# A third width for the first layer of an expert's unit: 128 columns when the unit holds one slot

## The chip, the cores and the metric

The kernel runs on one core of a Trainium2 chip. The metric is device time in microseconds (us), the median of a few executions. A core has TensorE (PE; its weight loads are listed apart as PEld), VectorE (DVE), ScalarE (ACT), GpSimd (POOL), a queue engine (SP), and 16 DMA engines. Each engine runs its own instruction stream in order, branches included; semaphores order the engines among each other.

## The reference

Three steps: a gated recurrence over time, a dense layer that takes the maximum of three products, and a layer that sends each of the 3072 tokens to one of eight experts.

```python
for t in range(S):                                   # recurrence, per batch and head
    state = alpha[:, :, t, :, None] * state + np.einsum('bhd,bhe->bhde', k[:, :, t], v[:, :, t])
    y[:, :, t] = np.einsum('bhd,bhde->bhe', q[:, :, t], state)

h = np.maximum(np.maximum(x @ w1, x @ w2), x @ w3)   # dense layer, 384 -> 768 -> 384
x = h @ w_out

e_idx = np.argmax(x @ w_gate, axis=1)                # experts, 384 -> 1024 -> 384
for e in range(E):
    mask = e_idx == e
    h = np.maximum(x[mask] @ w1[e], 0.0)
    out[mask] = gate_w[mask, None] * eom[mask, e, None] * (h @ w2[e])
```

The change touches the first product of the experts alone, `x[mask] @ w1[e]`.

## The kernel before

The first 446 us compute the recurrence and the dense layer; the change leaves them as they are. After them stands the expert layer. The tokens of an expert are cut into units of 256 tokens, held in slots of 128. The program is written for 20 units (`NU`), of which units 0 and 1 stand outside any branch, units 2 to 9 always run (`NV` is 10), and units 10 to 19 run only if the input has that many; `turn(u)` (L1447) calls the next turn inside a branch on the number of units (L1485), so that a run with fewer units jumps from the last one to the end of the program.

What an expert's last unit holds is its *kind*, worked out at run time (`units_e`, L876) and loaded into a register of each engine by `load_meta` (L925). Kind 0 is two slots (256 columns). Kind 2 is two slots and a rest of up to 64 tokens (256 + 64 = 320 columns). Kind 3 is a unit with at most 128 tokens: one slot. A rest that has no full unit before it is done elsewhere (`own`, L1095).

A turn of unit `u` does, in the order of each engine's program: the first layer `up(u)` (L1036); the split of the expert's second weights into a high and a low part, if the expert is new (`split2`, L676: ACT writes `w2H`, DVE subtracts and writes `w2L`); the gathers, transposes and first-weight splits for the next unit (skipped if there is none, L1465); the second layer of slot 0, `down_tile(u, 0)` (L1069); a tiny expert (`own`) in the turns of units 2 to 9; then the second layer of slot 1 and of the rest, `down_rest` (L1090), which for kind 3 is replaced by a one-column filler matmul into `psN` (`nothing`, L997). GpSimd then sends the finished rows to the output with an indirect DMA (`send`, L1039; `put`, L1043).

The first layer makes the 1024 hidden values in eight blocks `f` of 128. For each block, `up_one` (L1014) runs nine matmuls into one bank of PSUM: three slices of the 384 inputs, times the products high*high, high*low and low*high of weights and tokens, all in the single-pass type fp32r.

```python
        for k in range(3):
            for m, (w, x) in enumerate(((w1H, hi), (w1H, lo), (w1L, hi))):
                mm(ps, w[:, k, f * 128:(f + 1) * 128], x[:, k, :n], start=(k + m == 0), stop=(k + m == 4))
```

The weights stand still in the array (128 x 128, loaded anew for each matmul) and `n` columns of tokens stream past. `cut` (L1023) then applies the ReLU on ACT (L1024) and takes the low part on DVE (L1027). PSUM banks for these blocks come from a pool of three (`psM`). After block 2 stands the first piece of the split of the second weights, in a branch of its own (L1034, L1440).

Before the change a unit's first layer has two arms, chosen by `by_kind` (L1001): kind 2 takes 320 columns, every other kind takes 256. In the program the arm with 320 stands first, so units of kind 0 and 3 jump over it. A branch is an instruction of every engine that loaded the register: PE, ACT, DVE and POOL.

Of the kernel before, what the change touches and what calls it, by code (L numbers as in the profile page):

```python
# [24 lines left out]
DM, FF1, NE, FF2 = 384, 768, 8, 1024  # L25
# [14 lines left out]
LAST = 64  # L40
# [48 lines left out]
def layers(tc, pool, wk, K, general, *args):  # L89
    with ExitStack() as ctx:  # L90
        _layers(ctx, tc, pool, wk, K, general, *args)


def _layers(ctx, tc, pool_, wk, K, general, qk, al, a0, v, vT, w123, wout, gates, ew1, ew2, out):
# [547 lines left out]
    xg, cx, gate, chg, fetched, eos, kind = ({} for _ in range(7))  # L642
# [358 lines left out]
    def by_kind(u, arms, rest):  # L1001
        if not arms or u not in kind:
            return rest()
        (n, f), *more = arms.items()
        with tc.If(kind[u] == n) as c:  # L1005
            f()
        with c.Else():
            by_kind(u, dict(more), rest)
# [5 lines left out]
    def up_one(u, n, f):  # L1014
        hi, lo = cx[u % 2]
        w1H, w1L = C["w1"]
        ps = bank(psM, "M", "psM1")[:, :n]
# [3 lines that stand above are left out]
        return ps  # L1021

    def cut(ps, n, f):  # L1023
        nc.scalar.activation(chid(0, f, slice(0, n)), ps, AF.Relu)  # L1024
        for a, b, to in ((0, min(n, 256), 384), (256, n, 320)):
            if a < b:
                nc.vector.scalar_tensor_tensor(C["h"][f // 4][:, f % 4, to:to + b - a], ps[:, a:b], 0.0,  # L1027
                                               chid(0, f, slice(a, b)).bitcast(F32), op0=ALU.max, op1=ALU.subtract)

    def up_some(u, n, fs, split=False):  # L1030
        for f in fs:
            cut(up_one(u, n, f), n, f)
            if split and f == 2:
                fresh(u, split2, range(2))  # L1034

    def up(u):  # L1036
        by_kind(u, {2: lambda: up_some(u, 256 + LAST, range(NE), True)}, lambda: up_some(u, 256, range(NE), True))

    def send(y, p, c):  # L1039
        nc.gpsimd.indirect_dma_start(out=out[:, :], out_offset=bass.IndirectOffsetOnAxis(ap=sidx[:p, c:c + 1], axis=0),  # L1040
# [128 lines left out]
    if not general:  # L1169
# [90 lines left out]
        for i in range(3, NBLK):  # L1260
            order = batches if i > 3 else [(c, b) for b in (1, 0) for c in range(CPB)]
            n = len(order)
            d = (starts[i + 1] - starts[i]) / n
# [175 lines left out]
    def fresh(u, split, *a):  # L1439
        with tc.If(chg[u] == 1):  # L1440
            split(u, *a)
# [5 lines left out]
    def turn(u):  # L1447
# [4 lines left out]
        if u + 2 < NU:  # L1452
            load_expert(u + 2)
        up(u)
        fresh(u, split2, range(2, NE))
        if u == NF:
# [87 lines left out]
```

## Time and profile before

| | |
|---|---|
| median of 3 runs | 717.69 us (716.19 to 717.78) |
| the profiled execution's own time | 715.22 us |
| its span, first to last instruction | 713.5 us |
| PE, PEld busy | 692.7 us (97%), 655.0 us (92%) |
| DVE, ACT, POOL busy | 392.7 us, 288.7 us, 122.7 us |
| last unit's first layer on PE | 687.55 to 695.72 us |
| last unit's second layer on PE | 695.86 to 700.50 us |
| start of the last send on POOL | 704.77 us |

The page counts PE busy while any of its pipelined matmuls is under way, so the spacing of starts says more than the busy share: 72 matmuls of 256 columns, each 0.28 us long by itself, start within 8.17 us. A weight load is 0.19 us long, and loads overlap matmuls and each other. Rows that end in "xN" merge N instructions; the time beside them is from the first start to the last end.

### The profile page before, as it was taken

The numbers are of one execution on the slowest core, as the hardware profiler recorded it, in microseconds if no ns is written. First come the engines' busy times: TensorE is split into PE (matmuls) and PEld (weight loads), VectorE is DVE, ScalarE is ACT, GpSimd is POOL, SyncE is SP. The second block draws the span as 40 slices with busy tenths as digits, with TensorE's granted clock in tenths as the row PEclk, the third lists the DMA queues.
The fourth block names the chain that finished last, engine by engine and source line by source line (L and its number), as shares of the span: only waits on it lengthen the run. The fifth ranks groups of instructions, "written<-read, shape, count | busy, mean of one in ns | idle before, by whom it ended". The sixth has DMA issues, their size and how long they took to land. (4 is left out here: it accounts for less than half of the span.)

```text
span 713.5 us, 13995 instructions
## 1 busy us (share of the span) xinstructions
PE 692.7 (97%) x5097; PEld 655.0 (92%) x5097; DVE 392.7 (55%) x897; ACT 288.7 (40%) x755; POOL 122.7 (17%) x136
## 2 busy tenths in 40 slices
PE   8999999999999999999999999999999999999992
PEld 8888999999999999999999999999878899999992
DVE  7868887476955736826324365872215264225461
ACT  4345442555733533524323214333325364234451
POOL 1000000001111110111111114052132243332320
PEclk9999999999999999999999999999999999999997
DMA  9905310561510510500000015026566342135330
GB/s 248 380 24 182 107 60 1 147 192 46 152 43 13 138 42 21 131 34 9 13 23 10 22 30 226 23 69 233 196 223 228 121 137 61 58 97 178 128 131 21
DMA packets 23019, 74.88 MB, mean 105 GB/s; under 512 B 7915, under 2 KB 12085, under 8 KB 19841
## 3 DMA queue, kind: packets, MB, share of 16 engines
q1 hardware_dynamic: 17376, 60.95, 26.2%
q0 software_dynamic: 4384, 11.72, 5.2%
q8 instruction: 55, 0.90, 0.5%
q10 hardware_dynamic: 1152, 0.89, 0.5%
q14 instruction: 52, 0.42, 0.2%
HBM read 100.67 MB, written 9.94 MB: 155 GB/s over the span
## 5 line engine op out<-in xcount | busy, mean ns | idle before, releaser
L1020 PE MATMUL psM<-cx,w1H 128*128 128x256 f32 (+1 forms) x576 | 110.1, 290 | 0.0
L489 POOL TENSOR_TENSOR hL<-hm,hH 128x384 fp32r<-128x384 f32 x36 | 38.6, 1072 | 387.6 <-ACT hH L484 387.5
L463 PE MATMUL hps<-xH,wH 128*128 128x384 f32 x432 | 103.7, 347 | 0.4 <-ACT hm L467 0.2
L463 PE MATMUL hps<-xH,wL 128*128 128x384 f32 x432 | 98.5, 335 | 1.6 <-DVE wL L432 1.6
L1077 PE MATMUL psP<-w2H,ch 128*128 128x384 f32 x368 | 99.0, 340 | 0.2 <-issue 0.2
L463 PE MATMUL hps<-xL,wH 128*128 128x384 f32 x432 | 98.5, 335 | 0.0
L1020 PEld LDWEIGHTS psM<-cx,w1H 128*128 128x128 f32 x576 | 91.1, 188 | 0.2
L1027 DVE SCALAR_TENSOR_TENSOR ch<-psM,ch 128x256 fp32r<-128x256 f32 (+1 forms) x128 | 44.6, 371 | 82.5 <-ACT ch L1024 71.8
L1020 PE MATMUL psM<-cx,w1L 128*128 128x256 f32 (+1 forms) x288 | 83.3, 289 | 0.0
L463 PEld LDWEIGHTS hps<-xH,wH 128*128 128x128 f32 x432 | 74.1, 188 | 5.6 <-ACT hm L467 1.2
L463 PEld LDWEIGHTS hps<-xH,wL 128*128 128x128 f32 x432 | 76.9, 188 | 2.3 <-DVE wL L432 2.3
L463 PEld LDWEIGHTS hps<-xL,wH 128*128 128x128 f32 x432 | 77.2, 188 | 0.3 <-DVE xL L375 0.3
L1077 PEld LDWEIGHTS psP<-w2H,ch 128*128 128x128 f32 x368 | 66.8, 188 | 2.8 <-issue 2.1
L503 PE MATMUL ops<-wo,hH 128*128 128x400 f32 x258 | 68.2, 345 | 0.0
L470 DVE TENSOR_TENSOR hm<-hm,hps 128x384 f32<-128x384 f32 x48 | 26.4, 550 | 69.0 <-PE hps L463 55.4
L1024 ACT ACTIVATE ch<-psM 128x256 fp32r<-128x256 f32 (+1 forms) x96 | 38.3, 401 | 62.9 <-PE psM L1020 57.1
L1077 PE MATMUL psP<-w2L,ch 128*128 128x384 f32 x184 | 61.7, 335 | 0.1
L484 ACT CAST hH<-hm 128x384 fp32r<-128x384 f32 x43 | 22.0, 512 | 87.9 <-DVE hm L473 84.1
L1020 PEld LDWEIGHTS psM<-cx,w1L 128*128 128x128 f32 x288 | 54.5, 189 | 0.0
L1040 POOL DMA_INDIRECT out<-yo,sidx x27 | 29.5, 1092 | 113.5 <-ACT yo L1088 24.5
L503 PEld LDWEIGHTS ops<-wo,hH 128*128 128x128 f32 x258 | 47.2, 188 | 0.4
L503 PE MATMUL ops<-wo,hL 128*128 128x400 f32 x129 | 44.4, 344 | 0.0
(263 smaller groups left out, 1108.6 us busy)
## 6 DMA issues: line engine op xcount, KB each, us to landing
s1a<-in_ew SPq DMA_DIRECT2D x12, 1536.0 KB
s2a<-in_ew SPq DMA_DIRECT2D x12, 1536.0 KB
s1b<-in_ew SPq DMA_DIRECT2D x8, 1536.0 KB
s2b<-in_ew SPq DMA_DIRECT2D x8, 1536.0 KB
ws<-in_w SPq DMA_DIRECT2D x6, 1152.0 KB
at<-in_al SPq DMA_DIRECT2D x16, 336.9 KB
vt<-in_v SPq DMA_DIRECT2D x8, 576.0 KB
x2d<-xs SPq DMA_DIRECT2D x24, 192.0 KB
```

The costliest lines, as they stand in the source:

```text
L463: mm(ps, slab(a, f)[:, w, k], b[i][:, k], start=(n == 0), stop=(n == 8))
L470: nc.vector.tensor_max(m, m, ps)
L484: nc.scalar.copy(hH[i, f], m)
L489: (nc.gpsimd if not general and i > 1 else nc.vector).tensor_sub(hL[i, f], hps["m"], hH[i, f].bitcast(F32))
L503: mm(ps[:, :DM + NG], a[i, f][:, ts_], wo[f // 3][:, b, f % 3], start=(f + n == 0), stop=(f + n == 7))
L1020: mm(ps, w[:, k, f * 128:(f + 1) * 128], x[:, k, :n], start=(k + m == 0), stop=(k + m == 4))
L1024: nc.scalar.activation(chid(0, f, slice(0, n)), ps, AF.Relu)
L1027: nc.vector.scalar_tensor_tensor(C["h"][f // 4][:, f % 4, to:to + b - a], ps[:, a:b], 0.0, chid(0, f, slice(a, b)).bitcast(F32), op0=ALU.m ...
L1040: nc.gpsimd.indirect_dma_start(out=out[:, :], out_offset=bass.IndirectOffsetOnAxis(ap=sidx[:p, c:c + 1], axis=0), in_=y[:p], in_offset=Non ...
L1077: mm(ps[:, :DM], chid(x, f, slice(128 * t, 128 * t + 128)), w[:, f], start=(f + n == 0), stop=(f == NE - 1 and n == 2))
```

## The change

`up` no longer uses `by_kind`. It has three arms, written out as two nested branches: kind below 2 takes 256 columns and stands in front; in the other branch kind 2 takes 320 columns, and what is left, kind 3, takes 128.

```diff
     def up(u):
-        by_kind(u, {2: lambda: up_some(u, 256 + LAST, range(NE), True)}, lambda: up_some(u, 256, range(NE), True))
+        if u not in kind:
+            return up_some(u, 256, range(NE), True)
+        with tc.If(kind[u] < 2) as c:
+            up_some(u, 256, range(NE), True)
+        with c.Else():
+            with tc.If(kind[u] == 2) as d:
+                up_some(u, 256 + LAST, range(NE), True)
+            with d.Else():
+                up_some(u, 128, range(NE), True)
```

A matmul of the new arm has the same weights and the same number per block; it streams `x[:, k, :128]` in place of `x[:, k, :256]`, and `cut` handles 128 columns on ACT and DVE. The second layer of kind 3 reads slot 0 alone, in both versions. Lines from 1043 on stand nine lower in the changed file.

On ACT, in the turn of unit 11, where the arm with 320 columns ends; the names are PSUM banks of the first layer (`psM`), the hidden values (`ch`), and the staged and the split second weights (`s2a`, `w2H`). Before:

```order
L1024 ACTIVATE ch<-psM_9711 128x320
L1005 UNCONDITIONAL_BRANCH
L1024 ACTIVATE ch<-psM_9724 128x256
L1024 ACTIVATE ch<-psM_9736 128x256
L1024 ACTIVATE ch<-psM_9748 128x256
L1440 COMPARE_AND_BRANCH
L669 CAST w2H<-s2a 128x384 x2
```

and with the change:

```order
L1024 ACTIVATE ch<-psM_10731 128x320
L1043 UNCONDITIONAL_BRANCH
L1024 ACTIVATE ch<-psM_10744 128x128
L1024 ACTIVATE ch<-psM_10756 128x128
L1024 ACTIVATE ch<-psM_10768 128x128
L1449 COMPARE_AND_BRANCH
L669 CAST w2H<-s2a 128x384 x2
```

Behind the arm with 320 columns there now stands an arm with 128 in place of the one with 256; the split after block 2 keeps its place in it.

On PE, the same turn, the seam behind the first arm (`w1H`, `w1L` are the high and low first weights, `cx` the transposed tokens). Before:

```order
L1020 MATMUL psM_9711<-cx,w1H 128x320 x2
L1020 MATMUL psM_9711<-cx,w1L 128x320
L1005 UNCONDITIONAL_BRANCH
L1020 MATMUL psM_9724<-cx,w1H 128x256 x2
L1020 MATMUL psM_9724<-cx,w1L 128x256
```

and with the change:

```order
L1020 MATMUL psM_10622<-cx,w1H 128x256 x2
L1020 MATMUL psM_10622<-cx,w1L 128x256
L1040 UNCONDITIONAL_BRANCH
L1043 COMPARE_AND_BRANCH
L1020 MATMUL psM_10635<-cx,w1H 128x320 x2
L1020 MATMUL psM_10635<-cx,w1L 128x320
```

The arm with 256 now comes first, a second comparison stands behind it, and the unconditional branch at its end leads past two arms, where the branch at the end of the first arm led past one.

## Rows read from the trace of the kernel before

**Rows 1.** The page: busy time, share of the span, instructions of each engine.

```profile
PE 692.7 (97%) x5097; PEld 655.0 (92%) x5097; DVE 392.7 (55%) x897; ACT 288.7 (40%) x755; POOL 122.7 (17%) x136
```

**Rows 2.** PE, groups by form: line, operation, shapes, count, busy us, mean ns.

```profile
L1077 PE MATMUL psP<-w2H,ch 128*128 128x384 f32 x368 | 99.0, 340 | 0.2 <-issue 0.2
L1020 PE MATMUL psM<-cx,w1H 128*128 128x256 f32 x384 | 67.8, 280 | 0.0
L1077 PE MATMUL psP<-w2L,ch 128*128 128x384 f32 x184 | 61.7, 335 | 0.1
L1020 PE MATMUL psM<-cx,w1H 128*128 128x320 f32 x192 | 42.3, 308 | 0.0
```

**Rows 3.** Timeline of PE, the last unit: start us, us, instruction.

```profile
687.55 0.39 PE L1020 MATMUL psM<-cx,w1H 128*128 128x256 f32 x2
...
695.72 0.28 PE L999 MATMUL psN<-ident 128*128 128x1 f32 x2
695.86 0.42 PE L1077 MATMUL psP<-w2H,ch 128*128 128x384 f32 x1
...
697.40 0.44 PE L1077 MATMUL psP<-w2L,ch 128*128 128x384 f32 x1
```

**Rows 4.** Timeline of ACT and DVE, the last unit.

```profile
695.97 0.38 ACT L1024 ACTIVATE ch<-psM 128x256 fp32r<-128x256 f32 x1 [0.65 <-PE psM L1020]
696.25 2.57 ACT L669 CAST w2H<-s2a 128x384 fp32r<-128x384 f32 x6
700.75 0.58 ACT L1088 ACTIVATE yo<-psP,gate 128x384 f32<-128x384 f32 x1 [1.93 <-PE psP L1077]
689.85 0.82 DVE L1027 SCALAR_TENSOR_TENSOR ch<-psM,ch 128x256 fp32r<-128x256 f32 x2 [0.29 <-issue]
696.38 0.42 DVE L1027 SCALAR_TENSOR_TENSOR ch<-psM,ch 128x256 fp32r<-128x256 f32 x1 [0.61 <-ACT ch L1024]
696.78 2.90 DVE L670 TENSOR_TENSOR w2L<-s2a,w2H 128x384 fp32r<-128x384 f32 x6
```

**Rows 5.** Waits from 695 to 713 us: who waited for whom, us, times, longest.

```profile
POOL out L1040 <- ACTq L1485: 10.6, 1, 10.6
```

**Rows 6.** Timeline of PEld: weight loads of 128 columns beside few streaming columns.

```profile
99.87 0.74 PEld L448 LDWEIGHTS gps<-gt,wT 128*128 128x128 f32 x6 [0.40 <-ACT wT L440]
695.60 0.31 PEld L999 LDWEIGHTS psN<-ident 128*128 128x128 f32 x2
```

**Rows 7.** PE and PEld, groups by form: what bounds the new matmul.

```profile
L448 PE MATMUL gps<-gt,wT 128*128 128x16 f32 x36 | 4.6, 255 | 0.4 <-ACT wT L440 0.3
L1012 PE MATMUL psM<-s1b,xF 128*64 128x256 f32 x72 | 8.4, 383 | 0.0
L1083 PEld LDWEIGHTS psP<-w2L,ch 128*64 128x64 f32 x32 | 4.3, 134 | 0.0
L448 PEld LDWEIGHTS gps<-gt,wT 128*128 128x128 f32 x36 | 4.6, 191 | 1.0 <-ACT wT L440 1.0
```

**Rows 8.** ACT and DVE, groups by form: the cuts of the first layer.

```profile
L1024 ACT ACTIVATE ch<-psM 128x320 fp32r<-128x320 f32 x32 | 14.0, 438 | 24.9 <-PE psM L1020 23.9 <-ACT ch L1024 0.9
L1024 ACT ACTIVATE ch<-psM 128x256 fp32r<-128x256 f32 x64 | 24.3, 383 | 38.0 <-PE psM L1020 33.2 <-PE psT L981 2.2 <-ACT ch L1024 2.0
L1027 DVE SCALAR_TENSOR_TENSOR ch<-psM,ch 128x256 fp32r<-128x256 f32 x96 | 40.4, 423 | 82.5 <-ACT ch L1024 71.8 <-ACTq L1440 6.2 <-issue 3.0
L1027 DVE SCALAR_TENSOR_TENSOR ch<-psM,ch 128x64 fp32r<-128x64 f32 x32 | 6.8, 214 | 0.0
```

**Rows 9.** Branches of L1005 (684.8 to 687 us; all) and L1485: ns min/median/max, starts.

```profile
L1005 PEldq COMPARE_BRANCH  x1: 332/332/332, 685.3 to 685.3; - x1
L1005 PEldq COMPARE_BRANCH  x35: 66/207/431, 479.8 to 700.3; - x35
L1485 PEldq COMPARE_BRANCH  x4: 76/128/3489, 661.8 to 704.3; - x4
```

**Rows 10.** The page: a queue of instruction fetches, packets, MB, share of 16 engines.

```profile
q8 instruction: 55, 0.90, 0.5%
```

## Prediction

> **What bounds the kernel now.** I read the page first: TensorE is busy for 97% of the span and no other engine for more than 55% [rows 1]. So a change counts where it alters when TensorE finishes. Then the groups by form, to see how often the new arm will be taken. The 256-column rows of the high weights number 384, the 320-column rows 192 [rows 2]; a first layer has 48 of them (8 blocks, 3 slices, two products), so 8 units took 256 columns and 4 took 320. The second layer of slots 0 and 1 shows 368 + 184 = 552 matmuls [rows 2]; a slot takes 24, so 23 slots ran where 12 units have 24. Exactly one unit did one slot, and only that one enters the new arm.
>
> Which one, the timeline of the end tells [rows 3]: the last first layer is 256 columns wide, 687.55 to 695.72 us, and is followed by one slot of second layer and no other. The unit with one slot is the last of the program, so what its first layer gains or loses stands near the end, with no later unit to hide it.
>
> Then I followed that end through ACT and DVE [rows 4]. The last cut on ACT starts at 695.97; the six casts of the second weights follow it from 696.25, the six subtractions on DVE from 696.78 to 699.68. TensorE begins the second layer at 695.86, and has to take up again at 697.40 when the first of these subtractions has ended. ACT scales the result at 700.75. The last send goes at 704.77, and the waits put it down to ACT's branch at L1485 [rows 5], the jump over the unused turns. So the path is: last first layer on PE, cut and casts on ACT, subtractions on DVE, second layer on PE, scaling, far jump, send. It moves as a whole with the end of the last first layer.
>
> **The change part by part.** *The 72 matmuls of the last unit.* They start over 695.72 - 687.55 = 8.17 us, 0.1135 us each [rows 3]. Halving their columns helps only if columns are what sets that pace. Each of them also loads 128 columns of weights, and the trace has a place with next to nothing but such loads: the gate product at L448 streams 16 columns, and its six loads, each 0.191 us long, take 0.74 us [rows 6, 7], so they start (0.74 - 0.19) / 5 = 0.110 us apart. In front of the filler matmul of one column two loads take 0.31 us, 0.12 us apart [rows 6]. The duration fits: a load of 64 columns takes 134 ns and one of 128 takes 191 [rows 7], 57 ns for each 64 columns, 114 for 128. A matmul with 256 columns at 0.1135 us is therefore already at the pace of its own weight load. I take 0.110 us for one with 128: 72 x (0.1135 - 0.110) = 0.25 us gained.
>
> The bounds are far apart, as no fp32r matmul under 256 columns stands in the trace. The best would be half the pace, 0.057 us, a gain of 4.1 us. The worst is the plain fp32 path: its rows stand at 383 ns against 280 for the same 256 columns [rows 2, 7], 103 ns more, and such a product takes two of them. If 128 columns in fp32r fell to that, at two passes of 0.110 us, the layer would lose 72 x (0.220 - 0.1135) = 7.7 us. I choose the value nearest to the loads with 16 columns, since only these show what happens when streaming is short.
>
> The Trainium skill states the loading cost the same way: in "TensorE: Matmul & The Clock Gate", section "LDWEIGHTS (loading the stationary operand)", the columns divided by 1.2 give the nanoseconds, 107 for 128 columns; the gate product's 0.110 us agrees. That page of the Trainium skill, section "Back-to-back issue gap", gives pairs of load and matmul at 128 columns a sustained 81 ns, which would gain 72 x (113.5 - 81) = 2.3 us here. The loads of this trace start 110 ns apart, above that figure, and the trace decides.
>
> *The last matmul itself* is shorter by 128 columns: (308 - 280) / 64 = 0.44 ns a column [rows 2], 0.06 us. That shifts the last cut, so it counts: 0.06 us gained.
>
> *The cuts.* On ACT 438 - 383 ns for 64 columns [rows 8] makes 0.86 ns a column, so a cut falls from 0.38 to 0.27 us; on DVE (423 - 214) / 192 = 1.09 ns, from 0.42 to 0.28 us. Seven of eight lie beside TensorE's matmuls: ACT idles 0.65 us and DVE 0.61 us before their last ones [rows 4]. Behind the last ACT cut the casts start 0.28 us after the cut's own start, already before it ends, so its 0.11 us are worth between 0 and 0.11; I take 0. The first subtraction on DVE needs the first cast, so DVE's cut is worth 0.
>
> *The branches.* A unit of kind 2 or 3 now passes two comparisons. TensorE's sequencer took the last unit's branch at 685.3 us for 332 ns [rows 9], while the first matmul behind it started at 687.55 [rows 3]: 2.2 us of queued work lie over it, and one more branch at the median of 207 ns [rows 9] fits below it. It costs 0, and if that cover were gone, 0.33 us for each of five units (four of kind 2, one of kind 3), 1.7 us. On DVE the branch chain shows once: its first two cuts of the last unit start at 689.85 after 0.29 us of "issue" [rows 4]. A second comparison may add 0.2 us there. These cuts free the first PSUM bank of three, which TensorE wants for its fourth block at 687.55 + 27 x 0.1135 = 690.61; the first cut ended near 690.27, so 0.34 us are free, and its new length gives 0.14 back. It costs 0.
>
> *The order of the arms.* Units of kind 0 no longer jump at the start, but jump over two arms at the end. There are five: 8 layers of 256 columns less units 0 and 1, which have no branch, and the last. I take this at 0 (same 2 us of cover) and keep its other end as a rival.
>
> Sum: 0.25 + 0.06 = 0.3 us faster. The profiled execution took 715.22 us, 1.7 us beyond its span; by it the sum is 714.9. The three runs have a median of 717.69, from 716.19 up, so the profiled one lies below all of them and the likely value of a new median is a little below 717.4. I say 717.2 us.
>
> **The rivals.** *The new matmul runs at the speed of its columns.* At 0.057 us PE would save 4.1 us. Not all arrives: the fourth block would be due at 687.55 + 27 x 0.057 = 689.09, but the first bank comes free only at about 690.13 (DVE's 689.85 plus a cut of 0.28), so some 1.0 us is waited for. 717.69 - 3.1 gives 714.6. For it: loads and matmuls overlap in every row. Against it: the loads at 0.110 us beside 16 columns. The sustained 81 ns of the Trainium skill would land between, at 717.69 - 2.3 = 715.4. Chance 0.07.
>
> *The new matmul falls to the plain fp32 path.* 7.7 us more on the path make 725.4. It decides if 128 columns of fp32r take two passes; then the rows would also number 144 or be far over 280 ns. Against it: 256, 320 and 384 columns of this type all follow one line of 0.44 ns a column. For it: no narrower one was ever run here. Chance 0.06.
>
> *The longer jump leaves what is fetched.* This is the rival on the slow side that touches the most units. Instructions come by DMA in 55 packets of 0.90 MB, 16 KB each [rows 10]. A branch inside what is at hand takes TensorE up to 431 ns; the far jump at L1485 took 3489 [rows 9]. An arm holds 72 matmuls and 72 loads, so two arms are 288 instructions and more. If the jump over two behaves like the far one, it costs 3.5 - 2.2 = 1.3 us in each of five units, 6.4 us in all: 724.1. It decides as soon as a branch on PE takes over 2.2 us. Against it: jumps over one arm cost at most 0.43 us, and a target two arms ahead may still lie in the following packet. Chance 0.06.
>
> The Trainium skill has a rule on this: in "Runtime: NRT & Kernel Launch", section "Instruction fetch mechanics", a block holds 256 instructions, and a taken branch whose target is outside the current two blocks waits for a fetch. By it, as an estimate, a jump of about 300 leaves two blocks from (300 - 256) / 256 of the starting places, one in six, so one of the five jumps might: 1.3 us, 718.7. No row here shows such a jump.
>
> *The change does nothing at all*, because no unit has one slot, is excluded by the 23 slots.
>
> **How the numbers follow.** The forecast, a change too small to see, has 0.78; the three rivals 0.07, 0.06 and 0.06; 0.03 is left for what no row shows, such as a lower granted clock at the end. A measurement of this kernel can tell about 0.3%, 2.2 us, from no change. Faster is 0.09, the first rival and 0.02 of the forecast's scatter; slower 0.14, both slow rivals and 0.02 of what is left; same 0.77. The likeliest case alone spans 715.4 to 718.7: the three runs already lie 1.6 us apart, and its terms can be off by some 0.5 us. Reaching down to the first rival's 714.6, and up by the branches' 1.7 us at their longest, gives 714.6 to 719.3; the two slow rivals stay outside.
>
> **What would show it.** In the changed profile, 72 matmuls of 128 columns should start 0.108 to 0.114 us apart, with loads back to back, and the last first layer should last about 7.9 us. ACT's cuts there should take 0.27 us, DVE's 0.28, both idle longer before each. The last subtraction should end, and the last send start, about 0.3 us earlier against the start of that layer. PE's branches in `up` should stay under 0.5 us and PE without a gap at the ends of the 256-column arms. A pace near 0.06 or 0.2 us, or a gap there, proves the forecast wrong.

## The result, and the profile after

The changed kernel takes 720.11 us in the median of 20 runs (718.16 to 728.89); the kernel before took 716.51 us in 20 runs beside them (715.09 to 717.78). The ratio of the means is 1.0064, with a 95% interval of 1.0049 to 1.0079: 0.64% slower, some 4.6 us. 717.2 us, a little faster or the same, had been forecast. The spread changed as well: of the 20 runs, five take 723.22 us or more, where the kernel before never passed 719.56 us in any comparison made here.

The page of the profiled execution (723.22 us, span 721.5) hardly differs in its sums. Its rows for [rows 1] and [rows 10]:

```profile
PE 699.5 (97%) x5097; PEld 661.6 (92%) x5097; DVE 392.0 (54%) x897; ACT 288.3 (40%) x755; POOL 123.8 (17%) x136
...
q8 instruction: 61, 1.00, 0.6%
```

TensorE has as many matmuls as before and is busy 6.8 us longer, with six more packets of instructions fetched. Where the time went shows only in the expert layer. The sum of TensorE's waits from 480 to 700 us (who waited for what: us in total, times, longest):

```profile
PE psT L981 <- issue: 1.2, 1, 1.2
PE psT L981 <- DVEq L1449: 1.0, 1, 1.0
PE psM L1020 <- issue: 0.6, 1, 0.6
```

The same view of before has these two alone:

```profile
PE psP L1077 <- issue: 0.2, 1, 0.2
PE psH L1106 <- ACT hF L1102: 0.2, 1, 0.2
```

TensorE had no idle stretch over 0.25 us there; now it has these three, 2.85 us together. The timeline of TensorE places them: behind the 256-column arms of units 2 and 8, and ahead of unit 11's first layer (idle time before the row in brackets).

```profile
491.10 0.28 PE L1020 MATMUL psM<-cx,w1L 128*128 128x256 f32 x1
492.41 0.41 PE L981 MATMUL psT<-ident,xg 128*128 128x128 f32 x2 [1.03 <-DVEq L1449]
...
632.05 0.28 PE L1020 MATMUL psM<-cx,w1L 128*128 128x256 f32 x1
633.52 0.41 PE L981 MATMUL psT<-ident,xg 128*128 128x128 f32 x2 [1.20 <-issue]
...
690.37 0.44 PE L1020 MATMUL psM<-cx,w1H 128*128 128x128 f32 x2 [0.62 <-issue]
```

Unit 11's layer therefore starts at 690.37 us instead of 687.55 [rows 3], 2.82 us later: the three gaps. What stands ahead of them is in the branch rows of TensorE's queue (count, ns min/median/max, starts), which answer [rows 9]:

```profile
L1040 PEldq COMPARE_BRANCH  x14: 76/382/2912, 489.7 to 687.5; - x14
L1040 PEldq COMPARE_BRANCH  x1: 1757/1757/1757, 489.7 to 489.7; - x1
L1040 PEldq COMPARE_BRANCH  x1: 2912/2912/2912, 630.2 to 630.2; - x1
L1043 PEldq COMPARE_BRANCH  x1: 2492/2492/2492, 687.8 to 687.8; - x1
L1466 PEldq TENSOR_LOAD <-tiny x1: 316/316/316, 491.5 to 491.5; - x1
```

The jump at the end of unit 2's arm takes 1757 ns where 431 was the longest before. It starts at 489.7 while 1.7 us of matmuls are queued (their last ends at 491.38), but a register load, in program order behind the jump, now starts at 491.5 instead of 489.6, and a second one behind it; then come the transposes. So 1.03 us stand empty. Unit 3's jump takes 301 ns. Units 6 and 7 have jumps of 1292 and 1424 ns that are just covered, that is, queued matmuls run on until they end; unit 8's takes 2912, where 2.1 us are queued.

That these jumps wait for instructions can be read from the packets of the instruction queue, q8: one runs from 630.70 to 631.67 us, and unit 8's jump ends at 633.10. In all profiles of this case together, TensorE has 39 branches over 1.2 us that start between 470 and 700 us, and each ends 1.29 to 1.61 us after the end of such a packet.

The second loss is in the last first layer. The windows on L1020 in unit 11 (length; busy us and count of PE, of PEld; granted clock; DMA share; GB/s):

```profile
690.30:693.03 2.73, 2.66 (x24) 2.67 (x24) 1.00 0.03 6
693.03:703.60 10.57, 10.56 (x51) 10.37 (x49) 0.50 0.06 21
```

The first 24 matmuls run 0.111 us apart, as forecast. At 693.03 the granted clock falls from 1.00 to 0.50 (2.4 to 1.2 GHz), and the others run some 0.21 us apart. The layer takes 13.22 us instead of the 8.34 of before:

```profile
687.50:695.90 8.40, 8.34 (x72) 8.17 (x72) 1.00 0.08 28
```

The clock is back at 706.7 us, in the middle of the second layer, which takes 1.1 us more. ACT and DVE at the end, for [rows 4]:

```profile
703.68 0.28 ACT L1024 ACTIVATE ch<-psM 128x128 fp32r<-128x128 f32 x1 [1.64 <-PE psM L1020]
703.85 2.57 ACT L669 CAST w2H<-s2a 128x384 fp32r<-128x384 f32 x6
709.61 0.58 ACT L1097 ACTIVATE yo<-psP,gate 128x384 f32<-128x384 f32 x1 [3.18 <-PE psP L1086]
703.99 0.29 DVE L1027 SCALAR_TENSOR_TENSOR ch<-psM,ch 128x128 fp32r<-128x128 f32 x1 [1.63 <-ACT ch L1024]
```

The cuts shrink as forecast (0.28 and 0.29 us) and only wait longer. For this execution, then: gaps 2.8, layer 4.9, from layer to scaling 1.1; of this 8.8 us, 8.0 arrive in the span. In the typical run the clock seems not to fall there, though only this run's trace shows the layer: the nine runs with a mean clock of 0.992 or more take 718.16 to 719.55 us, some 2 to 3 us over before, the five with 0.988 or less take 723.22 to 728.89, and the six between take 720.10 to 721.44.

### The profile page after: what moved, and what is told of

It is laid out like the page before. It is cut to its first block, busy times and chain, and to the rows that moved or that the text cites. A ratio compares the mean times of both kernels' runs of the same rounds, so it can differ in the third digit from the quotient of the medians.

```text
span 721.5 us, 14047 instructions
## 1 busy us (share of the span) xinstructions
PE 699.5 (97%) x5097; PEld 661.6 (92%) x5097; DVE 392.0 (54%) x897; ACT 288.3 (40%) x755; POOL 123.8 (17%) x136
## 5 line engine op out<-in xcount | busy, mean ns | idle before, releaser
L1020 PE MATMUL psM<-cx,w1H 128*128 128x256 f32 (+2 forms) x576 | 114.5, 297 | 0.6 <-issue 0.6
L1020 PEld LDWEIGHTS psM<-cx,w1H 128*128 128x128 f32 x576 | 94.9, 196 | 1.1 <-issue 1.0
L1027 DVE SCALAR_TENSOR_TENSOR ch<-psM,ch 128x256 fp32r<-128x256 f32 (+2 forms) x128 | 43.7, 363 | 89.0 <-ACT ch L1024 79.0
L1020 PE MATMUL psM<-cx,w1L 128*128 128x256 f32 (+2 forms) x288 | 85.5, 297 | 0.0
L1024 ACT ACTIVATE ch<-psM 128x256 fp32r<-128x256 f32 (+2 forms) x96 | 37.7, 394 | 68.0 <-PE psM L1020 64.2
L1020 PEld LDWEIGHTS psM<-cx,w1L 128*128 128x128 f32 x288 | 56.9, 198 | 0.0
```

## The experiments

Theory at the start: the narrow layer makes the clock fall. Rival: the order of the arms and its longer jumps cost the time. The median of the kernel before beside each group of runs stood at 716.4 to 717.0 us. "Slower by" so many us is a difference of medians; the ratio, with its 95% interval in brackets, is the better measure and can differ a little from it.

**First group: one part of the change at a time.** 256 columns in the third arm, the rest as changed:

```diff
-                up_some(u, 128, range(NE), True)
+                up_some(u, 256, range(NE), True)
```

> The changed kernel with its three arms in the changed order, but 256 columns in the third arm as well: only the width of the last unit's 72 matmuls is undone. Theory (the granted clock): the narrow stretch is what makes TensorE's granted clock fall inside unit 11's first layer; here it stays at 1.00 until about 705 us, the 72 matmuls run 0.113 us apart, the first layer of unit 11 lasts 8.2 to 8.4 us again, and of the 4.6 us lost at most 0 to 2 us stay (716.5 to 718.5 us). Rival (order of the arms and longer jumps): the loss stays, 719.5 to 721.5 us, with gaps of PE ahead of units 2, 3, 6, 7, 8 or 11.

Measured: 718.90 us, ratio 1.0037 (1.0015 to 1.0058), 2.3 us slower without a narrow matmul. The rows of its jumps, and of the gap behind unit 8:

```profile
L1040 PEldq COMPARE_BRANCH  x15: 76/337/3262, 480.1 to 688.7; - x15
...
634.63 0.41 PE L981 MATMUL psT<-ident,xg 128*128 128x128 f32 x2 [1.56 <-issue]
```

So about half of the loss stays without narrow columns, with the jumps, against my theory. One of its 12 runs took 726.42 us at a mean clock of 0.983.

The old order with one more arm of 128 columns, tested second:

```diff
-        by_kind(u, {2: (320 columns)}, (256 columns))
+        by_kind(u, {2: (320 columns), 3: (128 columns)}, (256 columns))
```

> The kernel before with its order of arms (320 columns tested first, 256 last), and one more arm of 128 columns tested second: only the width is changed, no 256-column unit jumps over more arms than it did except for one more test. Theory (the granted clock): the clock falls to 0.50 some 2 to 4 us into unit 11's first layer, that layer lasts 12 to 14 us, and the time is 718.5 to 721.5 us. Rival (order of the arms and jumps): the clock may fall but costs little, 716 to 718 us.

Measured: 723.56 us, ratio 1.0086 (1.0059 to 1.0112). Both expectations miss. In the profiled run the clock holds to 713 us; now the 320-column arm ends in a jump over two arms, which takes 2217 to 3845 ns in units 4, 5, 9 and 10 and leaves a gap behind each. Besides, a gap of 1.85 us stands in the middle of unit 3's layer. The branch row and two of the five gaps:

```profile
L1005 PEldq COMPARE_BRANCH  x38: 63/213/3845, 482.1 to 694.9; - x38
...
548.80 0.41 PE L981 MATMUL psT<-ident,xg 128*128 128x128 f32 x2 [1.40 <-issue]
...
659.47 0.32 PE L981 MATMUL psT<-ident,xg 128*128 128x128 f32 x1 [1.82 <-issue]
```

Its gaps add up to 6.8 us, about the loss. So it is not the 256-column arm in particular: here the 320-column arm pays, since it now ends in the jump over two others.

Narrow columns in the five units with two tiles as well:

```diff
         with tc.If(kind[u] < 2) as c:
-            up_some(u, 256, range(NE), True)
+            up_some(u, 128, range(NE), True)
```

> The changed kernel with 128 columns also in the arm of the units with two tiles (units 2, 3, 6, 7 and 8); the first layer of their second tile is left out, and their second layer reads old values there. Theory (the granted clock): the granted clock falls to 0.50 in each of these five first layers as well, 2 to 4 us after its start, each layer grows from 8.2 to 12 to 14 us and drags a piece of its second layer, so the time is 740 to 755 us. Rival 1 (the fall belongs to the end of the program): the clock stays 1.00 in the five layers, they last 7.9 to 8.1 us, and the time is 718 to 721 us. Rival 2 (a narrow matmul with fp32 weights is slow whatever the clock): starts 0.2 us apart in rows at clock 1.00, 745 to 760 us.

Measured in one run: 715.14 us. (The kernel leaves out the first layer of those units' second tile, so its times alone count.) The windows on L1020 of unit 2 and of unit 11:

```profile
483.30:491.60 8.30, 8.15 (x72) 8.08 (x72) 1.00 0.69 249
687.50:695.80 8.30, 8.26 (x72) 8.12 (x72) 1.00 0.08 27
```

No layer lost the clock, not even unit 11's, ahead of which TensorE stood for 0.72 us. In this run six thin layers did not pull the clock down, and rival 2 falls as well. One run can't show how often they do; the 12 runs of the third group bear on that. Its jumps are long as well (1262 to 2377 ns behind units 2, 6, 7 and 8), but only unit 8's leaves a gap over 0.25 us, 0.65 us.

An arm with fewer loads: w1H is loaded once for hi and lo side by side (256 columns), w1L for hi alone:

```diff
+            mm(ps, w1H[:, k, f * 128:(f + 1) * 128], hi[:, k, :256], ...)
+            mm(ps[:, :128], w1L[:, k, f * 128:(f + 1) * 128], hi[:, k, :128], ...)
```

> The kernel before with its order of arms and an arm for one slot, tested second, that keeps the columns at 256 for one of two loads: lo's 128 columns are copied behind hi's, so the high half of the weights is loaded once and multiplies both (256 columns), and the low half multiplies hi alone (128 columns). From the second block on that is 6 loads for a block instead of 9, 51 instead of 72 in all; the two halves of a bank are added by ScalarE and VectorE. Theory (the granted clock, which holds as long as the engine's columns are not thinned to 128 throughout): clock 1.00 to the end of the layer, 51 loads at 0.112 us are 5.7 us instead of 8.2, and the time is 713.5 to 715.5 us. If the clock falls here too, some 25 loads and a part of the second layer run at half pace: 717 to 720 us. Rival (jumps and arms cost what was lost): 716.5 to 718 us at clock 1.00.

Measured: 720.58 us, ratio 1.0051 (1.0033 to 1.0069). The copy of lo waited on VectorE behind unit 10's last output, TensorE waited for it, and the clock fell 4.5 us into the layer:

```profile
687.80:692.30 4.50, 2.72 (x24) 2.58 (x23) 1.39 (x4) 1.59 (x4) 1.00 (x1) 1.00 0.08 27
692.30:695.70 3.40, 3.40 (x19) 3.40 (x18) 2.16 (x8) 2.11 (x8) 0.92 (x1) 0.50 0.09 28
```

(The columns are as above, with DVE, ACT and POOL behind PEld.) TensorE idled 1.78 of the first 4.50 us. That suggested a new theory: an idle stretch and the narrow layer together.

This run also bears on the jumps. Its arms stand in the order of the second run, and its 320-column arm ends in a jump over two others as well. But the new arm has 51 matmuls and 51 weight loads, so the jump passes 246 of these instructions where the second run's passes 288. All four of these jumps take 281 to 292 ns, and no gap stands behind them. Unit 4's:

```profile
L1005 PEldq COMPARE_BRANCH  x1: 292/292/292, 541.1 to 541.1; - x1
```

So it is not the number of arms that costs.

**Second group: three misses and one answer.** These were meant to put arms into the last unit alone, but stood in the code of the last unit that the program could have, the 20th, and the data stops at the 12th. None of the three arms was taken:

```diff
+        arms = {3: (128, 256 columns or the pair)} if u == NU - 1 else {}
+        by_kind(u, {**arms, 2: (320 columns)}, (256 columns))
```

> The kernel before, with the 128-column arm in the code of unit 11 alone and tested first there; units 2 to 10 keep the two arms and the order of before. What is asked: how much of the loss belongs to the branches of units 2 to 10, and how much to the narrow arm. If the gaps of PE behind units 2 and 8 (1.03 and 1.20 us) came from the longer jump at the end of the 256-column arm, they are gone, no branch of units 2 to 10 takes over 0.8 us, and a run whose clock holds takes 716 to 717 us. If the narrow stretch pulls the clock down in about half of the runs whatever stands ahead of it, the median is 717 to 719 us and the spread stays wide (up to 725 us and more). If the falling clock needs a gap of PE ahead of the stretch (0.62 us in the changed kernel), the spread is that of before and the median 716 to 716.6 us.

> The same program as the run above, with 256 columns in unit 11's own arm, so that only the width differs. Theory (branches of units 2 to 10 and narrow columns, each for itself): both are gone here, 716 to 717.2 us, as before. Rival (any change of the program's length shifts what is fetched, wherever it stands): 718 to 719 us with gaps of PE.

> The arm that loads the high half of the weights once for hi and lo (48 loads instead of 72), for unit 11 alone and tested first there, with the copy of lo moved ahead of unit 10's second layer. If the clock holds: 48 loads at 0.113 us are 5.4 us instead of 8.2, no gap inside the layer, 713.5 to 714.7 us. If the clock falls inside the layer as in the narrow arm, 716 to 719 us with a wide spread. If VectorE's and ScalarE's four operations for a block or the casts of w2 become the bound: layer 6 to 7.5 us, 714.7 to 716.5 us.

Measured: 715.80, 716.76 and 716.54 us, ratio 0.9998 in all three (widest interval 0.9983 to 1.0013). They test none of the theories. They show what a program that is longer behind the last unit costs: nothing.

The fourth had two arms with 256 in front:

```diff
+        with tc.If(kind[u] < 2) as c:
+            up_some(u, 256, range(NE), True)
+        with c.Else():
+            up_some(u, 256 + LAST, range(NE), True)
```

> Two arms as before in units 2 to 10, but with 256 columns in front as in the change, so that a 256-column unit jumps over one arm at its end, not over two; unit 11 as before. Theory (length of the jump): branches stay below 0.8 us, no gap of PE over 0.3 us, 716 to 717.2 us. Rival (the jump's place, at the end of the arm with little queued work left, costs whatever its length): gaps behind units 2, 3, 6, 7 or 8 as in the changed kernel, 718 to 719 us.

Measured: 719.43 us, ratio 1.0037 (1.0020 to 1.0053), without any gap over 0.25 us. By the same slip unit 11 took 320 columns: its layer lasts 10.72 us against 8.34, 2.4 of the 2.6 us. It was run again below.

**Third group: the arm in unit 11 alone, and another order.** The diff is that of the second group with `u == 11`.

> The kernel before with the 128-column arm in the code of unit 11 alone, tested first there, so that units 2 to 10 keep the branches of before. Theory (two causes): without the longer jumps there is no gap of PE over 0.3 us, and a run in which the granted clock holds takes 715 to 716.5 us; if narrow columns alone pull the clock down, some runs of the dozen are at 720 to 726 us with a mean clock under 0.988, and the median is 716.5 to 719 us. Rival (the fall needs the gap ahead of the layer, so the jumps are the only cause): all runs at 715 to 719 us, as with 256 columns in the run below.

> The same program with 256 columns in that arm: the width alone differs. Both theories: 716 to 717.3 us, spread as before.

Measured: 716.85 us with 128 columns (715.20 to 719.01, ratio 1.0002, 0.9987 to 1.0016) and 716.63 with 256 (1.0001, 0.9986 to 1.0016). The windows on L1020 in unit 11, first of the 128-column kernel, then of the 256-column one:

```profile
687.40:695.70 8.30, 8.15 (x72) 8.10 (x72) 1.00 0.09 29
```

```profile
689.20:697.70 8.50, 8.34 (x72) 8.24 (x72) 1.00 0.09 28
```

With the jumps of before in units 2 to 10 there is no gap, none of 12 runs is above 719.01 us (719.73 with 256 columns), and the narrow layer gains 0.19 us, too little to measure in the total. Unit 11's new arm does end in a jump over two arms of 144 matmuls and loads each, at no cost:

```profile
L1005 PEldq COMPARE_BRANCH  x1: 288/288/288, 693.5 to 693.5; - x1
```

> The arm with 48 loads instead of 72 (the high half of the weights loaded once for hi and lo) taken by unit 11, tested first there, lo copied ahead of unit 10's second layer. If the clock holds: the layer lasts 5.5 to 6 us instead of 8.3 and the time is 713.8 to 715 us. If the clock falls inside it in a part of the runs: 715 to 718 us with a wide spread. If ScalarE and VectorE (four operations of 0.25 to 0.31 us for a block, and the casts of w2) are the bound: the layer lasts 6 to 7.5 us, 715 to 716.3 us.

Measured: 718.93 us, ratio 1.0034 (1.0018 to 1.0050). 48 loads still take 8.0 us, since each block's copy, sum, relu and difference run one after the other on ScalarE and VectorE, 0.87 us a block, and TensorE waits for a bank, once for 1.11 us; in the profiled run the clock fell at 697.6 us, when the layer was over. The third expectation named this bound, but set it too low.

The rarest arm in front in every unit:

```diff
+        by_kind(u, {3: (128 columns), 2: (320 columns)}, (256 columns))
```

> The new arm in every unit as in the change, but tested first: 128, then 320, then 256 columns, so that no arm that units 2 to 10 take ends in a jump over two others (the 256-column arm ends without one, the 320-column arm jumps over one). Theory (length of the jump at an arm's end, with little queued work left to cover it): no gap of PE over 0.3 us behind a first layer, 715.5 to 717.5 us unless the clock falls in unit 11. Rival (three arms make the program too long, wherever the jumps stand): gaps as in the changed kernel, 718 to 721 us.

Measured: 717.11 us, ratio 1.0008 (0.9993 to 1.0022). No arm that units 2 to 10 take ends in a jump over two, and no gap stands behind a layer. One is left in the middle of unit 3's, as in the second run. No branch stands in it; one packet of instructions arrives between 509 and 512 us. What sets this gap is not shown:

```profile
511.90 0.40 PE L1020 MATMUL psM<-cx,w1H 128*128 128x256 f32 x2 [1.85 <-issue]
```

**Fourth group: the two places apart.** The change's three arms in unit 11 alone, with its 128 columns:

```diff
+        if u != 11:
+            return by_kind(u, {2: (320 columns)}, (256 columns))
         with tc.If(kind[u] < 2) as c:    # from here on as changed
```

> Units 2 to 10 as before; unit 11 alone has the change's three arms in the change's order (256, 320, 128), so that it makes the two jumps ahead of its 128 columns. Theory (two prices, jumps in units 2 to 10 and, ahead of unit 11, a gap of PE that pulls the clock down in a part of the runs): the gap ahead of the layer is 0.3 to 1 us, most runs take 716.5 to 717.7 us, and one to four runs of the dozen take 720 us and more. Rival (the clock falls by itself whatever stands ahead, or only after the earlier gaps): no run over 719.5 us.

Measured: 721.82 us, ratio 1.0091 (1.0057 to 1.0125). Three of six runs took 717.90 to 719.78 us, all above the 716.5 to 717.7 expected for most, and three 723.87 to 727.05 at mean clocks of 0.984 and less; the profiled run is not one of these three. In the profiled run (717.90) the clock held in unit 11, but the gap can be read from the second of the two jumps ahead of the layer and from its first matmul:

```profile
L1042 PEldq COMPARE_BRANCH  x1: 3398/3398/3398, 686.7 to 686.7; - x1
...
690.20 0.44 PE L1020 MATMUL psM<-cx,w1H 128*128 128x128 f32 x2 [1.50 <-ACT ylo L1074]
```

The branch ends at 690.1 us, and the matmul starts behind it, whatever the row names as releaser.

The opposite: the change's arms in units 2 to 10, and unit 11 with its 128 columns tested first:

```diff
+        if u == 11:
+            return by_kind(u, {3: (128 columns), 2: (320 columns)}, (256 columns))
```

> The other half: units 2 to 10 have the change's three arms in the change's order, unit 11 tests its 128 columns first and makes no jump ahead of them. Theory: gaps of PE of 0.8 to 1.6 us behind units 2 and 8 remain, so the time is 717.7 to 719 us, and no run is over 722 us, since nothing stands still ahead of unit 11's narrow layer. Rival (all of the loss is at unit 11): 716 to 717.3 us.

Measured: 719.16 us (718.76 to 721.92), ratio 1.0055 (1.0038 to 1.0072). 2.5 us slower by the medians, 3.9 by the ratio, and no run above 722. Its gaps behind units 2 and 8:

```profile
493.60 0.41 PE L981 MATMUL psT<-ident,xg 128*128 128x128 f32 x2 [1.21 <-DVEq L1450]
...
635.22 0.41 PE L981 MATMUL psT<-ident,xg 128*128 128x128 f32 x2 [1.15 <-issue]
```

The jumps ahead of them take 2318 and 2872 ns. In the same kernel unit 3's takes 301 and unit 11's, over two arms as well, 316.

Two arms with 256 in front, unit 11 as before:

> Units 2 to 10 have the two arms of before with 256 columns in front, as in an earlier run, and unit 11 keeps the kernel of before and so its 256 columns (there it took 320). A 256-column unit now ends in a jump over one arm instead of two. Theory (length of the jump): no gap of PE over 0.3 us, 716 to 717.2 us. Rival (place of the jump at the arm's end): 718 to 719 us with gaps behind the 256-column units.

Measured: 716.63 us, ratio 1.0007 (0.9997 to 1.0018). Nothing is lost that can be measured. The branches of TensorE in `up`:

```profile
L1039 PEldq COMPARE_BRANCH  x14: 76/244/2999, 480.3 to 663.2; - x14
```

The five jumps at the ends of 256-column arms, over one arm, take 174 to 324 ns. The longest branch (2999 ns, at 530.7 us, ahead of unit 4's layer and over the one arm of 256 columns) stands under the long second layer and leaves a gap of 0.55 us, the only one. So in units 2 to 10 what is lost comes with the longer jump at the end of a layer, not with the order of two arms. But length is not all: this branch is long over one arm, unit 11's jump is short over two, and unit 3's takes 301 ns in all four kernels with the change's arms there, whose units 2, 6, 7 and 8 take 1262 to 3262. Where a jump stands in the program matters too, and these runs do not separate the two.

The operands turned round, in unit 11 alone:

```diff
+                    mm(ps, x[:, k, :128], w[:, k, 512 * a:512 * a + 512], ...)
+            nc.scalar.activation(h[:, 512 * a:512 * a + 512], ps, AF.Relu)
+                nc.tensor.transpose(ps[:, 128 * f:128 * f + 128], h[:, ...], ident)
```

> An arm for one slot, in unit 11 alone and tested first, that turns the operands round: the 128 tokens are the loaded operand and 512 columns of the weights stream past them, 18 matmuls and 18 loads instead of 72 and 72; the result has tokens on the partitions, so 8 transposes and one cut per four blocks follow. By the pace of the 384-column matmuls of the second layer (0.173 us) a 512-column one takes about 0.23 us: 4.2 us, and 8 transposes at 0.11 us 0.9 us, with one or two waits of 0.5 to 1 us for ScalarE between. Theory (with few loads PE is bound by its columns, the clock holds): the layer lasts 5.3 to 6.5 us instead of 8.3, 713.5 to 715.2 us. Rival (the casts of w2 bound the end whatever the first layer takes, or the waits eat the gain): 715.8 to 717.2 us.

Measured: 715.07 us (713.88 to 717.32), ratio 0.9982 (0.9968 to 0.9995): the only kernel that beats both. The timeline of its end on TensorE:

```profile
692.65 0.40 PE L1044 MATMUL psM<-w1H,cx 128*128 128x512 f32 x1
692.88 0.60 PE L1051 MATMUL psM<-ident,hF 128*128 128x128 f32 x4
693.78 0.66 PE L1051 MATMUL psM<-ident,hF 128*128 128x128 f32 x4 [0.30 <-ACT hF L1045]
...
695.18 0.42 PE L1098 MATMUL psP<-w2H,ch 128*128 128x384 f32 x1
```

From the layer's first matmul (688.75) to the second layer it takes 6.43 us, where [rows 3] give 695.86 - 687.55 = 8.31.

**Fifth group.** The run with jumps in unit 11 alone, with 256 columns:

> Units 2 to 10 as before; unit 11 alone has the change's three arms in the change's order with 256 columns in the third as well, so the jumps and the gap of PE ahead of its layer (1.5 us in the run with 128 columns) stay and the width alone differs from that run, of which 3 of 6 were at 723.9 to 727.1 us. Theory (gap and thin columns together pull the clock down): no run over 721 us, 717 to 718.5 us. Rival (the gap alone does): a third or more of the runs at 722 us and more.

Measured: 717.65 us (716.79 to 720.24), ratio 1.0022 (1.0012 to 1.0033). The gap ahead of the layer is 1.39 us, and the time is 1.2 us longer by the medians; none of 12 runs passes 720.24 us, where three of six did by 3.6 us and more with 128 columns.

```profile
688.92 0.50 PE L1020 MATMUL psM<-cx,w1H 128*128 128x256 f32 x2 [1.39 <-ACT ylo L1074]
```

In this place the long runs came with the gap and the thin columns together, and with neither alone.

> The arm with operands turned round (18 matmuls of 512 columns and 8 transposes) in the code of every unit, tested first. It is about 40 instructions long on TensorE, against some 150 of the other arms. Theory (a jump is free as long as it passes over one long arm and little more): no gap of PE over 0.6 us in units 2 to 10, 715 to 716.3 us, as with the arm in unit 11 alone (715.07 us). Rival (any third arm costs): gaps in units 2 to 10, 716.7 to 719 us.

Measured: 719.62 us, ratio 1.0039 (1.0024 to 1.0055). The rival falls, and the theory's time with it. Units 2 to 10 have no gap over 0.25 us; unit 11's short arm (52 matmuls, transposes and loads, not about 40) ends in a jump over two long ones, and TensorE runs out of queued work:

```profile
L1005 PEldq COMPARE_BRANCH  x1: 3288/3288/3288, 693.6 to 693.6; - x1
...
697.62 0.59 PE L999 MATMUL psN<-ident 128*128 128x1 f32 x2 [3.41 <-issue]
```

In this run the granted clock stood at 0.50 from 696.9 to 703.7 us besides, so the gap is not the whole loss. The same arm with the same jump stands in the kernel of 715.07 us, whose branches on L1005 take 431 ns at most up to 700 us:

```profile
L1005 PEldq COMPARE_BRANCH  x36: 66/209/431, 481.5 to 699.3; - x36
```

Its place in the program differs.

## Why the prediction was wrong, step by step

The forecast of 717.2 us set out from 717.69, the median of three runs; 20 runs gave 716.51. Against that it expected a gain of 0.3 us, and 3.6 were lost by the medians, 4.6 by the ratio.

*One unit, the last, takes the new arm; its loads set the pace.* Right. 72 matmuls of 128 columns stand in unit 11, 0.111 us apart while the clock held. The layer by itself gained 0.19 us (8.34 to 8.15) of the 0.31 forecast for it and its last matmul. The rivals "speed of the columns" and "plain fp32 path" fell with this.

*The cuts are worth nothing.* Right, in length and in worth.

*The order of the arms costs 0 (same 2 us of cover).* This is the step that failed. It was wrong twice: the jump over two arms takes 1.3 to 2.9 us where 0.43 was the longest known, in four of five units, and the cover was less than the 2.2 us counted ahead of unit 11, 1.7 us in unit 2 and 2.1 in unit 8, less the register loads that queue behind the jump (two in unit 2, one in unit 8). The rival "the longer jump leaves what is fetched" had the mechanism; its price was too high, 1.3 us in each of five units, since only units 2 and 8 show a gap, 1.03 and 1.20 us. I gave it 0.06, on the argument that the target might lie in the following packet. The run with the jumps in units 2 to 10 alone sizes it: 2.5 us by the medians, 3.9 (2.7 to 5.2) by the ratio.

The Trainium skill, in "Runtime: NRT & Kernel Launch", section "Instruction fetch mechanics", has a taken branch wait when its target lies outside the two current blocks. The estimate drawn from it, one jump of five, was too mild: four of five are over 1.2 us. That a jump's price hangs on its place is borne out by the two kernels with the short arm (3288 ns, and at most 431 on the same line), and that the long ones wait for a fetch by the packets they end behind.

*One more branch ahead of unit 11 fits under 2.2 us of queued work.* Also wrong: it was priced at 207 ns, and the branch at L1043, the second of two jumps in a row, takes 2492, and TensorE stands for 0.62 us. By the 256-column run with these jumps that costs 1.2 us where the gap is 1.39.

*A lower granted clock at the end* had 0.03, without a price. In the one traced run it costs 4.9 us in the layer; that it also makes the other four of the five runs of 723 to 729 us is read from their times and mean clocks alone. Neither the gap (none of 12 runs) nor the thin columns (none of 12) brought such times in unit 11; both together did in three of six. That they do so in the changed kernel itself is argued from these runs, not shown; why some runs escape stays open, as does the one run of 726.42 us with 256 columns throughout, which may be a fall without thin columns.

## What to carry to other kernels

A new arm of a branch is paid for by those who do not take it: count the instructions that the jump at each arm's end passes, the work queued ahead of it on the engine, and the register loads behind it; put the rare arm where no common arm must jump over it. Halving columns buys next to nothing where each matmul brings its own weight load (0.19 of 8.34 us); turning the operands round, so that few loads serve many columns, did (6.43 us instead of 8.31).

## What the runs showed of the hardware

A long branch on TensorE is a wait for instructions: all 39 over 1.2 us (470 to 700 us, all profiles) end 1.29 to 1.61 us after a packet of instructions has come. Jumps at the end of a layer in units 2 to 10 past 246 matmuls and loads or fewer took at most 379 ns in all profiles; past 288, 20 of 24 took 1262 ns or more. Place counts besides: a jump past the same two arms took at most 431 ns in one program and 3288 in another, which differs in that every unit has the short arm, so in how much code stands ahead of it.

In some runs the granted clock drops early too, far ahead of the code that was changed: to 0.50 from 58.8 to 62.2 us in a profiled run of a kernel whose new arm is never taken, and between 11 and 16 or 58 and 64 us in seven other profiled runs. By an estimate from that row, such a stretch at half pace costs up to 1.7 us. So not every lower mean clock belongs to unit 11.
